# Gated linear attention and a max-out layer: a new opening, eight items transposed on PE, and matmuls on zeros in its gaps

## The chip, the cores and the metric

The kernel runs on one core of a Trainium2 chip. The metric is the device time of one execution in microseconds (us); the time before is the median of three runs, 171.43 us (169.94 to 171.87). The profile is of one execution of 170.57 us, whose span from first to last instruction is 168.3 us. PE is TensorE (matmuls), DVE VectorE, ACT ScalarE, POOL GpSimd, SP the engine whose queue issues all transfers.

## The reference

Inputs q, k, v and alpha have the shape (4, 8, 768, 48): 4 batches, 8 heads, 768 steps, head size 48, in float32. A gated linear attention runs over the steps, and its output of 3072 tokens x 384 goes through a max-out layer:

```python
for t in range(S):
    state = alpha[:, :, t, :, None] * state + np.einsum('bhd,bhe->bhde', k[:, :, t], v[:, :, t])
    y[:, :, t] = np.einsum('bhd,bhde->bhe', q[:, :, t], state)
x = np.ascontiguousarray(attn_out.transpose(0, 2, 1, 3)).reshape(B * S, H * D)
h1 = x @ w1      # w1, w2: 384 x 1024
h2 = x @ w2
g = np.maximum(h1, h2)
out = g @ w_out  # 1024 x 384
```

## The kernel before

**Items.** The attention works on 12 items, each 256 steps of one batch with all 8 heads; two steps lie side by side in a partition. An item loads alpha, q, k and v (384 KB each). ACT takes the logarithm of alpha (`ln`, L418), DVE adds the two steps (`su`, L425), PE forms running sums with triangular matrices (`cs`, L435 to L443), ACT takes exponentials (`en`, `ep`, `gg`), POOL multiplies k by en (`kt`, L474), DVE multiplies q (`qt`, L480), POOL casts v (`vc`, L489). Then q and k must be transposed. For the items in `TURN`, the first five, PE does that with 16 matmuls against the identity (L510) and ACT or DVE copies the result out of PSUM; for the other seven, two DMA transposes in the SP queue do it (L522). PE then forms the states (`kv`, L540), the scores (`sc`, L620); DVE masks them (`pt`, L628), PE forms y (L674) and ACT or DVE writes it to xT, transposed for the next layer (`xe`). DVE and POOL carry the states on from item to item (`w`, `T`, `t32`).

**Max-out.** max(h1, h2) is relu(x(w1 - w2)) + x w2, so the kernel keeps wd = w1 - w2 and m = w2 w_out, which PE computes once (L360, L392). Tokens come in chunks of 128; groups of 2 or 3 chunks go through `h` (L701, 24 matmuls with 256 or 384 columns), a relu each on ACT or DVE (L711, L709), and then for every chunk 3 matmuls with m (L726) and 8 with w_out (L728). An output chunk is evicted from PSUM (`ev`) and stored (`st`, L736).

**Order.** No loop fixes the order. All operations are handed to a planner (`Plan`, with `add` and `run`): each has a duration per engine it may run on, what it depends on, buffers it takes and releases, and a priority, where a smaller number goes first. `run` builds one fixed order per engine, which the chip then executes in order. Among the buffers are the 8 PSUM banks, in pairs ("A", for the attention) or singly ("M"). An operation of item n has a priority of about 100 n, a group g has 3000 + 100 g, so attention goes before groups. Loads have about -1000, stores -1500, DMA transposes -2000; all three share the SP queue. The planner limits how far ahead of the transfers SP issues (`LEAD`) and counts `xfer` us for each. Item 0 is loaded first, then the twelve loads of the weights (w2, w1, w_out in four pieces each), then items 1 to 11. There are 20 load buffers of 3 KB per partition and 6 output buffers.

Of the kernel before, what the change touches and what calls it, by code (L numbers as in the profile page):

```python
# [24 lines left out]
class Op:  # L25
    __slots__ = ("name", "engs", "emit", "deps", "takes", "uses", "prio", "mode", "xfer", "eng", "start", "end", "seen", "n")


class Plan:
# [4 lines left out]
    LEAD = 3.0  # L34

    def __init__(self, pools):
        self.free = dict(pools)
        self.banks = [True] * 8
        self.ops = []

    def room(self, takes):
        need = {}
        for b in takes:
            need[b.pool] = need.get(b.pool, 0) + 1
        for p, k in need.items():
            if p == "A":
                if self.pair() is None:
                    return False
            elif p == "M":
                if not any(self.banks):  # L50
                    return False
            elif self.free[p] < k:
                return False
        return True
# [7 lines left out]
    def take(self, b):  # L62
# [3 lines left out]
        elif b.pool == "M":  # L66
            free = [i for i in range(7, -1, -1) if self.banks[i]]
            half = [i for i in free if not self.banks[i ^ 1]]
            b.at = (half or free)[0]
            self.banks[b.at] = False  # L70
        else:
            self.free[b.pool] -= 1

    def give(self, b):
        if b.pool == "A":
            self.banks[b.at] = self.banks[b.at + 1] = True
        elif b.pool == "M":
            self.banks[b.at] = True
        else:
            self.free[b.pool] += 1  # L80

    def add(self, name, engs, emit, deps=(), takes=(), uses=(), prio=0.0, mode=None, xfer=0.0):
        o = Op()
        o.name, o.engs, o.emit, o.prio, o.mode, o.xfer = name, engs, emit, prio, mode, xfer
# [10 lines left out]
    def run(self):  # L95
        idle = {e: 0.0 for e in self.LAT}
        mode = None
        dma = 0.0
        order = []
# [3 lines left out]
        while waiting:  # L103
# [9 lines left out]
            for o in waiting:  # L113
# [6 lines left out]
                if ready is None:  # L120
# [6 lines left out]
                for e, dur in o.engs.items():  # L127
# [6 lines left out]
                    key = (o.prio, o.n)  # L134
                    if e not in best or key < best[e][0]:
                        best[e] = (key, o, dur)
            done = set()
            for e, (key, o, dur) in sorted(best.items(), key=lambda x: x[1][0]):
# [5 lines left out]
                if e == "PE" and o.mode != mode:  # L144
                    dur += self.SWITCH
                    mode = o.mode
# [3 lines left out]
                if e == "SP":  # L150
                    dma = max(dma, t + 1.3) + o.xfer
# [17 lines left out]
def kernel(  # L169
# [23 lines left out]
    WMAX = 384  # L193
    TURN = (0, 1, 2, 3, 4)
# [3 lines left out]
    NLD = 20  # L198
# [14 lines left out]
    plan = Plan({"ld": NLD, "en": 2, "loga": 2, "qk": 3, "pt": 4, "w": 4, "t32": 3, "gg": 3, "g": 2, "g16": 3, "outs": 6})  # L213
# [24 lines left out]
    def setup_pool1(eng):  # L238
        make_upper_triangular(nc, u16, val=1.0, diag=True)
        nc.gpsimd.memset(half1, 0.0)  # L240
# [7 lines left out]
        make_identity(nc, ident16)  # L248

    def setup_dve1(eng):  # L250
        nc.vector.memset(s16s[0][:, :, D:64], 0.0)
        nc.vector.memset(s16s[1][:, :, D:64], 0.0)
        nc.vector.tensor_sub(out=cmat, in0=u16, in1=half1)
        nc.vector.memset(cmat[0:64, 64:128], 0.0)
        nc.vector.tensor_sub(out=us16, in0=u16, in1=ident16)
        nc.vector.tensor_scalar_mul(out=nid16, in0=ident16, scalar1=-1.0)
        for i in range(2):
            nc.vector.memset(qkts[i].rearrange("p a j h d -> p (a j h) d")[:, :, D:64], 0.0)

    def setup_pool2(eng):  # L260
        for t in v16s:
            nc.gpsimd.memset(t.rearrange("p j h d -> p (j h) d")[:, :, D:96], 0.0)

    def setup_dve2(eng):
# [7 lines left out]
        nc.vector.memset(qkts[2].rearrange("p a j h d -> p (a j h) d")[:, :, D:64], 0.0)  # L272

    def setup_pool3(eng):
        for t in T16s:
            nc.gpsimd.memset(t, 0.0)

    s_p1 = plan.add("setp1", {"POOL": 2.6}, setup_pool1, prio=-100)
    s_d1 = plan.add("setd1", {"DVE": 2.6}, setup_dve1, deps=[s_p1], prio=-100)
    s_p2 = plan.add("setp2", {"POOL": 1.6}, setup_pool2, deps=[s_p1], prio=-90)  # L280
    s_d2 = plan.add("setd2", {"DVE": 1.3}, setup_dve2, deps=[s_d1], prio=-80)
    s_p3 = plan.add("setp3", {"POOL": 1.5}, setup_pool3, deps=[s_p2], prio=80)


    LX = 1024 * 20.5 / 16e3
    ld = {}

    def add_load(n, which, prio):
        src = {"a": alpha, "q": q, "k": k, "v": v}[which]
        b, c = divmod(n, NDB)  # L290
        buf = Buf("ld")

        def emit(eng):
            t = A["ld", n, which] = ldp.tile([128, H, 2 * D], FP32, tag="ld", name=which + "f")
            nc.sync.dma_start(  # L295
                out=t, in_=src[b, :, c * 256 : (c + 1) * 256, :].rearrange("h (p j) d -> p h (j d)", j=2)
            )

        ld[n, which] = (plan.add(f"ld{which}{n}", {"SP": 0.65}, emit, takes=[buf], prio=prio, xfer=LX), buf)

    WX = 384 * 1024 / 400e3
    wl = {}

    def add_wload(name, i, prio):
# [3 lines left out]
        def emit(eng):  # L308
            if name == "wo":
                t = ldp.tile([128, 2, DM], FP32, tag="ld", name="wof")  # L310
                nc.sync.dma_start(
                    out=t, in_=src[i * 256 : (i + 1) * 256, :].rearrange("(s p) d -> p s d", p=128)
                )
            else:
                t = ldp.tile([128, 3, 256], FP32, tag="ld", name=name + "f")
                nc.sync.dma_start(
                    out=t, in_=src.rearrange("(s p) f -> p s f", p=128)[:, :, i * 256 : (i + 1) * 256]
                )
            A["w", name, i] = t

        wl[name, i] = (plan.add(f"ld{name}{i}", {"SP": 0.5}, emit, takes=[buf], prio=prio, xfer=WX), buf)

    seq = [("d", 0)] + [("w2", i) for i in range(4)] + [("w1", i) for i in range(4)] + [("wo", i) for i in range(4)]
    seq += [("d", n) for n in range(1, ND)]
    pos = 0
    for name, i in seq:
        if name == "d":
            for w in "aqkv":
                add_load(i, w, -1000 + pos)
                pos += 1  # L330
        else:
            add_wload(name, i, -1000 + pos)
# [11 lines left out]
    w2c, wdc, woc, ptc = [], [], [], []  # L344
    for i in range(4):
        o, b = wl["w2", i]
        w2c.append(plan.add(
            f"w2c{i}", {"ACT": 0.83, "DVE": 0.55, "POOL": 1.25},
            lambda eng, i=i: cast(eng, w216[:, :, i * 256 : (i + 1) * 256], A["w", "w2", i]),
            deps=[o], uses=[b], prio=50 + i))  # L350

    for i in range(4):
        ps = Buf("M")

        def emit(eng, i=i, ps=ps):
            tp = A["wtp", i] = bank(ps, 384).bitcast(FP16).rearrange("p (u m) -> p u m", u=6)
            for u in range(2):
                for s in range(3):
                    f = 2 * i + u
                    nc.tensor.transpose(tp[:, 3 * u + s, :], w216[:, s, f * 128 : (f + 1) * 128], ident16)  # L360

        tr = plan.add(f"wtp{i}", {"PE": 0.34}, emit, deps=[w2c[i], s_p1], takes=[ps], prio=60 + i, mode=0)
        ptc.append(plan.add(
            f"wtc{i}", {"DVE": 0.6, "ACT": 0.8},
            lambda eng, i=i: cast(eng, w2T[:, 2 * i : 2 * i + 2, :].rearrange("p u m -> p (u m)"),
                                  A["wtp", i].rearrange("p u m -> p (u m)")),
            deps=[tr], uses=[ps], prio=61 + i))

    for i in range(4):
        o1, b1 = wl["w1", i]  # L370
        o2, b2 = wl["w2", i]

        def emit(eng, i=i):
            e = nc.vector if eng == "DVE" else nc.gpsimd
            e.tensor_sub(out=wd16[:, :, i * 256 : (i + 1) * 256], in0=A["w", "w1", i], in1=A["w", "w2", i])

        wdc.append(plan.add(f"wd{i}", {"DVE": 1.0, "POOL": 1.9}, emit, deps=[o1, o2], uses=[b1, b2], prio=70 + i))
    for i in range(4):
        o, b = wl["wo", i]
        woc.append(plan.add(  # L380
            f"woc{i}", {"ACT": 0.83, "DVE": 0.55, "POOL": 1.25},
            lambda eng, i=i: cast(eng, wo16[:, 2 * i : 2 * i + 2, :], A["w", "wo", i]),
            deps=[o], uses=[b], prio=74 + i))

    mc = []
    for s in range(3):
        ps = Buf("M")

        def emit(eng, s=s, ps=ps):
            mp = A["mp", s] = bank(ps, DM)  # L390
            for f in range(NF):
                nc.tensor.matmul(mp, lhsT=w2T[:, f, s * 128 : (s + 1) * 128], rhs=wo16[:, f, :],  # L392
                                 start=(f == 0), stop=(f == NF - 1))

        mm = plan.add(f"mp{s}", {"PE": 1.3}, emit, deps=ptc + woc, takes=[ps], prio=78 + s, mode=0)
        mc.append(plan.add(f"mc{s}", {"ACT": 0.48, "DVE": 0.5},
                           lambda eng, s=s: cast(eng, m16[:, s, :], A["mp", s]), deps=[mm], uses=[ps], prio=79 + s))
# [5 lines left out]
    def attention(n):  # L403
# [10 lines left out]
        loga_b = Buf("loga")  # L414

        def e_ln(eng):
            t = A["loga", n] = wk.tile([128, H, 2, D], FP16, tag="loga", name="loga")
# [367 lines left out]
```

## Time and profile before

| | busy us | share of span | instructions |
|---|---|---|---|
| PE | 134.8 | 80% | 2144 |
| DVE | 77.8 | 46% | 136 |
| ACT | 84.1 | 50% | 155 |
| POOL | 71.5 | 42% | 113 |

| view | what it says |
|---|---|
| chain that ended last | PE 49%, DMA 26%, DVE 7%, POOL 5% |
| SP queue | last input load issued at 103.4 us; 14 DMA transposes from 63.6 to 113.8 us |
| transfers | 23.59 MB read, 4.72 MB written |

The busy share of an engine is an average over the whole span. The rows with 40 digits cut the span into slices of 4.2 us, so that stages can be told apart. [...]matmuls overlap; what one costs in a stream is the distance from one start to the next.

### The profile page before, as it was taken

The page shows a single profiled execution, that of the slowest core. Times are in us where ns is not written, and L with a number is a line of the kernel's source. Part 1 is how long each engine was busy: PE and PEld are TensorE (multiplying, and loading weights), DVE is VectorE, ACT ScalarE, POOL GpSimd, SP SyncE. Part 2 cuts the span into 40 slices and gives each one's busy share as a digit, 9 for nine tenths or more (in the row PEclk, how much of TensorE's full clock was granted, in tenths as well). Part 3 has the DMA queues.
Part 4 walks back from the last instruction along what each step waited for, and adds up shares of the span by engine and source line. Part 5 has one row for each costly group of instructions (what it writes and reads, how often), then busy time and mean ns, then how long its engine had stood idle before and what let it go on. Part 6 is the DMA issues. An engine that isn't in the chain of part 4 may idle for free.

```text
span 168.3 us, 5032 instructions
## 1 busy us (share of the span) xinstructions
PE 134.8 (80%) x2144; PEld 89.6 (53%) x2144; DVE 77.8 (46%) x136; ACT 84.1 (50%) x155; POOL 71.5 (42%) x113
## 2 busy tenths in 40 slices
PE   0058599967884868969599894789989999999991
PEld 0047466745673645636256672545645666667660
DVE  3939922849678856618269564651930000001100
ACT  3255657453836549533563365262145482926342
POOL 7647900959794696781706467094100000000000
PEclk9999999999999699999879999699999999999999
DMA  5999999999999999999999999967210212103112
GB/s 142 265 346 348 370 280 238 274 247 266 310 241 277 251 257 247 197 268 246 200 237 208 235 254 219 263 78 156 90 51 0 93 47 76 68 25 117 47 47 93
DMA packets 72469, 32.29 MB, mean 192 GB/s; under 512 B 65280, under 2 KB 72448, under 8 KB 72448
## 3 DMA queue, kind: packets, MB, share of 16 engines
q1 hardware_dynamic: 72448, 31.99, 81.7%
q8 instruction: 16, 0.26, 0.7%
q14 instruction: 5, 0.04, 0.1%
HBM read 23.59 MB, written 4.72 MB: 168 GB/s over the span
## 4 chain that ended last, share of the span: by engine, by line
PE 49%; DMA 26%; DVE 7%; POOL 5%; SPq 4%; issue 4%; ACT 3%; DVEq 0%; ACTq 0%; POOLq 0%
PE PS L701 13%; PE PS L728 13%; DMA af<-in_alpha_dram 11%; DMA qk<-qkt 8%; PE PS L674 6%; PE PS L726 5%; DMA vf<-in_v_dram 4%; DMA w2f<-in_moe_w_dram 3%; PE PS L392 3%; SPq L295 3%; DVE pt L628 2%; PE PS L620 2%; POOL qkt L474 2%; PE PS L435 2%; PE PS L510 1%
## 5 line engine op out<-in xcount | busy, mean ns | idle before, releaser
L701 PE MATMUL PS<-xT,wd 128*128 128x384 f16 (+1 forms) x216 | 37.6, 319 | 3.9 <-ACT xT L338 2.6
L728 PE MATMUL PS<-wo,g 128*128 128x384 f16 x192 | 37.2, 326 | 0.0
L628 DVE TENSOR_TENSOR pt<-PS,mask 128x1024 f16<-128x1024 f32 x24 | 28.1, 1217 | 3.8 <-PE PS L620 3.5
L701 PEld LDWEIGHTS <-wd 128*128 128x128 f16 x216 | 20.3, 99 | 15.8 <-issue 4.7
L474 POOL TENSOR_TENSOR qkt<-kf,en 128x768 f16<-128x768 f32 x12 | 21.7, 1813 | 14.9 <-ACT gg L460 6.9
L711 ACT ACTIVATE g<-PS 128x384 f16<-128x384 f32 (+1 forms) x55 | 24.5, 458 | 6.3 <-PE PS L701 5.9
L709 DVE TENSOR_SCALAR g<-PS 128x384 f16<-128x384 f32 (+1 forms) x17 | 7.8, 493 | 37.8 <-PE PS L701 37.1
L338 ACT COPY outs<-PS 128x384 f32<-128x384 f32 x23 | 11.0, 478 | 28.2 <-PE PS L728 28.2
L728 PEld LDWEIGHTS <-g 128*128 128x128 f16 x192 | 18.1, 98 | 11.8 <-ACT g L711 0.2
L418 ACT ACTIVATE loga<-af 128x768 f16<-128x768 f32 x12 | 10.1, 843 | 18.8 <-DMA af<-in_alpha_dram 18.8
L620 PE MATMUL PS<-qk 48*64 48x128 f16 x384 | 9.5, 233 | 9.6 <-DMA qk<-qkt 5.1
L435 PE MATMUL PS<-s,cmat 128*128 128x384 f16 x24 | 8.4, 385 | 9.2 <-DVE s L425 8.5
L726 PE MATMUL PS<-m,xT 128*128 128x384 f16 x72 | 15.7, 326 | 0.0
L489 POOL CAST v<-vf 128x768 f16<-128x768 f32 x12 | 9.9, 823 | 13.0 <-DMA vf<-in_v_dram 12.8
L575 POOL TENSOR_TENSOR T<-w,gg 48x192 f16<-48x192 f32 x24 | 12.9, 539 | 4.3 <-DVE w L600 3.4
L620 PEld LDWEIGHTS <-qk 48*64 48x64 f16 x384 | 7.3, 115 | 13.1 <-issue 12.2
L480 DVE TENSOR_TENSOR qkt<-qf,PS 128x384 f16<-128x384 f32 x24 | 12.0, 546 | 4.0 <-DMA qk<-qkt 4.0
L452 ACT ACTIVATE en<-PS 128x768 f32<-128x768 f32 x12 | 9.7, 807 | 8.3 <-PE PS L443 8.1
L674 PE MATMUL PS<-pt,v 64*64 64x128 f16 x576 | 12.0, 233 | 0.1
L338 ACT CAST xT<-PS 128x384 f16<-128x384 f32 x13 | 7.6, 585 | 7.5 <-PE PS L701 4.5
L340 DVE CAST xT<-PS 128x384 f16<-128x384 f32 x11 | 6.5, 588 | 10.2 <-PE PS L701 5.4
L674 PEld LDWEIGHTS <-v 64*64 64x64 f16 x576 | 9.7, 116 | 1.6 <-issue 0.6
(66 smaller groups left out, 162.1 us busy)
## 6 DMA issues: line engine op xcount, KB each, us to landing
af<-in_alpha_dram SPq DMA_DIRECT2D x12, 384.0 KB, 6.1
qf<-in_q_dram SPq DMA_DIRECT2D x12, 384.0 KB, 5.8
kf<-in_k_dram SPq DMA_DIRECT2D x12, 384.0 KB, 5.7
vf<-in_v_dram SPq DMA_DIRECT2D x12, 384.0 KB, 6.0
out_dram<-outs SPq DMA_DIRECT2D x24, 192.0 KB, 1.9
w2f<-in_moe_w_dram SPq DMA_DIRECT2D x4, 384.0 KB, 5.9
w1f<-in_moe_w_dram SPq DMA_DIRECT2D x4, 384.0 KB, 7.8
wof<-in_moe_w_out_dram SPq DMA_DIRECT2D x4, 384.0 KB, 8.0
```

Of the source, the lines that this page charges most:

```text
L338: nc.scalar.copy(out=out, in_=in_)
L435: nc.tensor.matmul(t[:, g, 0:384], lhsT=cmat, rhs=s16[:, 4 * g : 4 * g + 4, 0:D].unsqueeze(2).to_broadcast([128, 4, 2, D]), start=True, st ...
L474: e.tensor_mul(out=hjd(qkts[i3], 1), in0=A["ld", n, "k"].rearrange("p h (j d) -> p h j d", j=2), in1=A["en", n].rearrange("p g (h j d) -> ...
L480: nc.vector.tensor_mul(out=hjd(qkts[i3], 0)[:, 4 * g : 4 * g + 4], in0=A["ld", n, "q"].rearrange("p h (j d) -> p h j d", j=2)[:, 4 * g : 4 ...
L575: e.tensor_mul(out=T16s[m % 4][o : o + 48, :, 48 * u : 48 * u + 48], in0=w_[o : o + 48], in1=g_[o : o + 48])
L620: nc.tensor.matmul(t[64 * x : 64 * x + 64, u, c0 : c0 + 128].rearrange("p (j m) -> p j m", j=2), lhsT=qk[o : o + D, 1, j, r, 64 * x : 64 * ...
L628: nc.vector.tensor_mul(out=t.rearrange("p u r c -> p (u r) c"), in0=A["sc", n, hf].rearrange("p u (r c) -> p (u r) c", r=2), in1=mask.rear ...
L674: nc.tensor.matmul(dst, lhsT=lhsT, rhs=rhs, start=(x, u) not in begun, stop=ends[x, u] == i, skip_group_check=True)
L701: nc.tensor.matmul(t[:, 0:W], lhsT=wd16[:, s, f * 128 : (f + 1) * 128], rhs=xT[:, s, a0 : a0 + W], start=(s == 0), stop=(s == 2))
L711: nc.scalar.activation(out=o, in_=i, func=ACTF.Relu)
L726: nc.tensor.matmul(A["op", t0], lhsT=xT[:, s, t0 : t0 + 128], rhs=m16[:, s, :], start=(s == 0), stop=False)
L728: nc.tensor.matmul(A["op", t0], lhsT=A["g16", g][:, f, i * 128 : (i + 1) * 128], rhs=wo16[:, f, :], start=False, stop=(f == NF - 1))
```

## The change

The change replaces the opening and retunes the planner:

- Items 0 to 7 are transposed on PE (`TURN`), items 8 to 11 by DMA.
- The weights come in six loads, w2, w_out and w1 by halves, between items 0, 1 and 2. Alpha and k share a load buffer, and so do q and v (10 buffers of 6 KB). m is built from two halves.
- Items 0 and 1 are worked in two halves of four heads (`SPLIT`), so that the first half can begin when half of alpha is there. Their k multiply is on DVE.
- Set-up work moves from POOL to DVE; the mask is built after the first sum.
- `FILL`: up to 60 matmuls on a tile of zeros, 128 x 512, with the lowest priority, which the planner may place where it foresees PE idle up to 24 us of its own count. Their result isn't used. They are there to keep PE's clock from falling to half. 55 of them are in the order of the built kernel.
- All groups have two chunks (`GROUPS`). Their priority is that of the item three later (`LAG`) instead of behind all attention. Stores go behind all loads (-100); there are 7 output buffers.
- In the planner, buffers are handed out in turn, PE is counted at half speed until it has been busy for 4 us (`WARM`), and several durations are set anew.

```diff
+TURN = (0, 1, 2, 3, 4, 5, 6, 7)
+SPLIT = (0, 1)
+LOADS = (0, ("w2", 0), ("wo", 0), ("w1", 0), 1, ("w2", 1), ("wo", 1), ("w1", 1), 2, 3, 4, 5, 6, 7, 8, 9, 10, 11)
+GROUPS = (2,) * 12
+LAG = 3.0
+FILL = (60, 24.0)
...
-    LEAD = 3.0
+    LEAD = 4.5
+    WARM = 4.0
...
-    TURN = (0, 1, 2, 3, 4)
...
-    NLD = 20
+    NLD = 10
...
-        for i in range(2):
-            nc.vector.memset(qkts[i].rearrange("p a j h d -> p (a j h) d")[:, :, D:64], 0.0)
-
-    def setup_pool2(eng):
-        for t in v16s:
-            nc.gpsimd.memset(t.rearrange("p j h d -> p (j h) d")[:, :, D:96], 0.0)
...
-    def setup_pool3(eng):
-        for t in T16s:
-            nc.gpsimd.memset(t, 0.0)
...
+    nfill, tfill = FILL
+    if nfill:
+        fz = constp.tile([128, 512], FP16)
+        fset = plan.add("fz", {"DVE": 0.2}, lambda eng: nc.vector.memset(fz, 0.0), prio=-120)
+        fb = Buf("M")
+        for i in range(nfill):
+            plan.add(f"fill{i}", {"PE": 0.21}, lambda eng: nc.tensor.matmul(bank(fb), lhsT=fz[:, 0:128], rhs=fz, start=True, stop=True,
+                                                                            skip_group_check=True),
+                     deps=[fset], takes=[] if i else [fb], uses=[fb] if i else [], prio=1e6 + i, mode=0, until=tfill)
...
-    LX = 1024 * 20.5 / 16e3
+    LX = 1024 * 25.5 / 16e3
...
+        split = n in SPLIT
+        parts = [(0, 4), (4, 8)] if split else [(0, 8)]
...
+            ke = {"DVE": 0.1 + 0.82 * F} if split else {"POOL": 0.1 + 1.72 * F}
...
-            ck = plan.add(f"dk{n}", {"SP": 1.2}, lambda eng: e_tr(eng, 1), deps=[kt], takes=[qkb], prio=-2000 + P, xfer=1.15)
...
+            cks.append(plan.add(f"dk{n}", {"SP": 1.2}, lambda eng: e_tr(eng, 1), deps=kts, takes=[qkb], prio=-2000 + P, xfer=1.6))
...
-        P = 3000 + 100 * g
+        P = 100.0 * ((c0 + nch - 1) // 2 + LAG)
...
-            plan.add(f"st{g}.{i}", {"SP": 0.65}, e_st, deps=[ev], uses=[ob], prio=-1500 + g, xfer=0.52)
+            plan.add(f"st{g}.{i}", {"SP": 0.65}, e_st, deps=[ev], uses=[ob], prio=-100 + g, xfer=0.52)
...
-    for g, nch in enumerate((2, 3, 3, 3, 3, 3, 3, 2, 2)):
+    for g, nch in enumerate(GROUPS):
```

## The prediction

> **What bounds the kernel now.** I read the slice rows of the page first, because a share over the whole span mixes stages here.
>
> ```profile
> PE   0058599967884868969599894789989999999991
> PEclk9999999999999699999879999699999999999999
> GB/s 142 265 346 348 370 280 238 274 247 266 310 241 277 251 257 247 197 268 246 200 237 208 235 254 219 263 78 156 90 51 0 93 47 76 68 25 117 47 47 93
> ```
>
> A slice is 4.2 us. Up to slice 26 (109 us) the DMA engines move 200 to 370 GB/s without a pause and PE has gaps; after that hardly anything is moved and PE is full. So there are two stages: until about 118 us PE is fed by transfers, then it works off a backlog. The stretches and waits (name, total us, times, longest) say the same:
>
> ```profile
> 8.50:30.00 21.50, 17.31 (x216) 12.71 (x216) 11.85 (x19) 13.58 (x20) 9.79 (x8) 1.00 1.10 315
> ...
> 118.00:165.00 47.00, 45.80 (x443) 28.93 (x431) 6.60 (x8) 23.41 (x54) 0.32 (x1) 1.00 0.16 58
> ```
>
> ```profile
> ACT loga L418 <- DMA af<-in_alpha_dram: 18.8, 12, 3.4
> ...
> PE PS L435 <- DVE s L425: 8.5, 1, 8.5
> ...
> PE PS L620 <- DMA qk<-qkt: 5.1, 3, 3.1
> ```
>
> ACT waits 18.8 us for alpha; PE waits 8.5 us once at the start and 5.1 us for the DMA transposes. The chain that ended last has these in the middle of the run:
>
> ```profile
> 62.00 6.75 DMA af<-in_alpha_dram
> ...
> 87.96 7.05 DMA qk<-qkt
> ...
> 100.26 5.76 DMA qk<-qkt
> ...
> 134.29 3.41 PE PS L701 x21
> ```
>
> Alpha and the transposed q and k take turns as the last releaser: both go through the one SP queue. The last line gives a price: 21 matmuls of 384 columns in 3.41 us, 0.163 us each.
>
> **How much PE work there is.** I priced PE's matmuls by their start-to-start times in undisturbed places of the timeline: 384 columns 0.163 us, 256 columns 0.109 (21 in 2.29), a score set of 32 0.57, a y of 16+48 matmuls 1.37, a state set of 32 0.37, a transpose 0.062 (16 in 1.0), a decay block (L435, L438, L443) 0.66. Summed over the kernel before this is 118.6 us, of a span of 168.3. By that scale PE does 45.5 us of work from 117.6 to 164.9 (rate 0.96), but from 61.6 to 102.9 only 32.4 (0.785), and from 27.6 to 117.6 only 64.0 of 90 (0.71). About 26 us of the span are lost in that 90 us stretch; that is what a change of staging can win.
>
> [...] L435 starts 0.32 us apart from its follower at 8.5, 55.5, 83.6 and 107.4 us, and 0.16 where PE was busy before. [...] The inputs' rows are 384 B, and the trace has 346 to 370 GB/s while weights move and about 263 (mean of slices 7 to 14) while inputs do. [...]
>
> **The change part by part.**
>
> *Transposes.* Items 5, 6 and 7 move from DMA to PE. Removed: 6 of 14 DMA transposes (1.4 us each in the SP queue, 4.3 us to landing), and with the new order the other 8 all come after the last load. Added: 48 PE transposes x 0.062 = 3.0 us of PE, and 6 copies of 0.68 (DVE) or 1.01 us (ACT), about 5 us on engines that are 46% and 50% busy. PE's sum becomes 121.7 us.
>
> *Loads.* The bytes are the same (23.6 MB). In before 8.25 MB stand ahead of and with item 2's alpha, which landed at 30.5; the new order has the same bytes there, so 30.5 again. It needs ln 0.84, sum 0.40 and some 0.5 of hand-overs: item 2's decay matmuls can start at 32.3. After that nothing but loads is on the queue: 1.573 MB an item at 263 GB/s is 6.0 us, item 3 at 38.3, item 11 at 86, where before still issued loads at 103.
>
> *Stores.* The instruction order has the first store behind all 54 input issues, and 7 output buffers. Chunk 7 (the eighth) has 55.4 us of PE work ahead of it: 32.3 + 39.7 = 72 at full rate; item 11's alpha lands near 84.5, its v 4.5 us later, and a load is issued some 6 us before it lands (the median of before): the last near 83, the first store behind it. So from 72 to about 85 finished chunks wait in PSUM: 7, then 8 (62.2 of work, 79), 9 and perhaps 10, up to four banks of eight: a new wait, longer by what the loads are late. Behind the waiting evictions stand the relus on ACT and DVE, and PE waits for those. I cost it at 0 to 6 us.
>
> *Groups of two items' chunks.* 288 matmuls of 256 columns (31.4 us) replace 144 of 384 and 72 of 256 (31.3): nothing. 96 relus of 0.38 to 0.42 for 72 of 0.38 to 0.56: 38 for 34 us on ACT and DVE, beside PE.
>
> *Priority.* A group's work now stands by the item three later, not behind all attention: in PE's order 15.7 us of work are ahead of item 2, then 22.7, 31.3, 37.1, 46.5, 56.0 ahead of items 3 to 7. An item is about 9.7 us of PE work ((121.7 - 5.4 for the weights)/12) against 6.0 of loading. So after item 2 the loads run ahead: item 3 is allowed at 38.3 and is reached at 39.3 at the earliest; by item 6 the slack is 63.1 against 56.3.
>
> *Opening.* Splitting items 0 and 1, the multiplies by en on DVE (two 1.81 us POOL operations become four of about 0.55 us on DVE), weights in six transfers, set-up moved from POOL to DVE (before's took until 8.05, with one DVE operation on 128x128 lasting 3.78 us): all of it ends ahead of item 2 at 32.3, which waits for its bytes, so on the path it is worth nothing by itself, but it must fit: 15.7 of work and 55 matmuls on zeros[...]. They are in PE's fixed order, so data that come earlier than the order foresees wait behind some of them[...]. Their use is a warm clock; cold stretches of before in the opening cost PE 2 to 3 us that were hidden.
>
> *Sum.* End = 32.3 + (108.0 - 15.7)/r + 13.7 + 3.4 + 2.3. 108.0 is the work up to item 11's y, 13.7 what follows and runs at full rate as in before, 3.4 the tail from the last matmul to the span's end (164.9 to 168.3), 2.3 the difference of time and span. r is PE's rate while attention and groups mix: the one unknown. Undisturbed stretches of before give 0.83 (61.6 to 73.7), 0.97 (95.1 to 102.9), 0.96 (from 117.6). With a backlog three items deep I take 0.93: 51.7 + 99.2 = 150.9, said as 151.
>
> **The rivals.** *A. Hand-overs or held PSUM banks (r 0.80 to 0.87).* For it: PE waits for xT, pt and qk copies in before, 0.3 to 2.1 us each, and the queue of stores. Against: an item costs DVE 4.6 us (sum 0.40, q 1.1, masks 2.4, states 0.7), ACT 2.6 (ln, two exps, gg) and either of them 7.1 (copies of q and k 1.7, xT 1.2, relus 3.2, outputs 1.0): 7.2 each, against PE's 9.7. Time 158 to 167. *B. Slower.* If before's mixed stage is slow because of the hand-overs between engines and not because of DMA, r stays at 0.71: 51.7 + 130 = 182; even 0.76 gives 173. Against: the chain has DMA where PE waits longest. *C. Better than thought.* r 0.98 or more and item 2's bytes 2 us earlier[...]: 142 to 145. *D. The gain is hidden anyway*, because PE works off a backlog at the end in both: but the sum of PE work is 118.6 against 168.3, so idle time is on the path.
>
> **Numbers.** The main case (146 to 157) 0.62, A 0.22, C 0.07, B 0.09 (a sliver of A and B falls within 1%). Range 144 to 165: it leaves out B, the far end of A and half of C. Faster 0.88, same 0.03, slower 0.09.
>
> **What would show it.** PE's digits at 9 from slice 8 on; no alpha or qk landing among PE's or the chain's long pieces after 33 us; last load issued by 88; no cold L521 after 35 us; item 2's decay matmuls at 31 to 34. Wrong if PE idles over 15 us after 33, if ACT or DVE stands waiting for stores around 75 to 92 with PE behind it, or if item 2 starts after 36.

## The result, and the profile after

The changed kernel takes 152.6 us, the median of four runs (152.01 to 153.17), against 171.35 us for the kernel before on the same chip: a ratio of 0.892, 95% interval 0.885 to 0.899. The ratios of this document leave out runs over 1.5% above the fastest of the same kernel; the medians include them. The profiled run's span is 151.3 us. The slices are now 3.78 us wide:

```profile
PE   6999989699999999999998988999989699999991
PEclk9999999999999999999999999999999999999999
GB/s 117 272 333 375 258 245 366 304 246 269 268 252 247 267 244 261 210 262 236 234 252 217 276 263 145 311 254 153 176 61 98 88 74 123 56 0 108 101 3 104
```

PE is at 90% or more in all but nine of the 40 slices, in the opening partly with the matmuls on zeros, and the clock row shows no slice in which the clock is lowered: its mean is 1.000 (the trace records it from 5.3 us on only; before that a matmul on zeros takes 0.42 us, right after it 0.22, as shown below). The transfers move 210 to 276 GB/s in most slices up to 90 us, as before: the same bytes at the same pace, but PE has far fewer gaps while they come. The three stretches that the prediction's sum speaks of (length, PE, PEld, DVE, ACT, POOL with instructions, clock, DMA share, GB/s):

```profile
8.50:34.10 25.60, 23.09 (x392) 15.38 (x392) 20.46 (x38) 15.14 (x31) 11.10 (x16) 1.00 1.04 306
34.10:134.20 100.10, 95.85 (x1800) 69.32 (x1798) 64.00 (x114) 55.94 (x113) 51.41 (x74) 1.00 0.84 200
134.20:148.10 13.90, 13.84 (x103) 9.58 (x99) 3.99 (x9) 5.67 (x13) 0.00 (x0) 1.00 0.16 58
```

The waits of PE from 33 us on (us in total, times, longest) are all that is left of before's:

```profile
PE PS L787 <- DVE xT L400: 1.7, 3, 0.6
PE PS L787 <- ACT xT L398: 1.2, 2, 0.7
PE PS L787 <- ACT g L797: 0.5, 1, 0.5
PE PS L787 <- DVE pt L714: 0.3, 1, 0.3
PE PS L760 <- issue: 0.2, 1, 0.2
```

That is 3.9 us, none of it on a transfer. In the kernel before, PE waited 5.1 us for the transposes alone. Of ACT's twelve waits for a load of alpha, 18.8 us before, one is left, for the first load of all. The chain that ended last has no DMA in its shares of the span (second fence):

```profile
ACT loga L502 <- DMA ldf<-in_alpha_dram: 1.5, 1, 1.5
```

```profile
PE 87%; DVE 6%; ACT 2%; issue 1%; POOL 1%; ACTq 0%; POOLq 0%
```

### The profile page after: what moved, and what is told of

The parts are those of the page before. It is cut to its first block, busy times and chain, and to the rows that moved or that the text cites. A ratio compares the mean times of both kernels' runs of the same rounds, so it can differ in the third digit from the quotient of the medians.

```text
span 151.3 us, 5429 instructions
## 1 busy us (share of the span) xinstructions
PE 140.1 (93%) x2319; PEld 97.4 (64%) x2319; DVE 94.4 (62%) x187; ACT 82.0 (54%) x167; POOL 64.6 (43%) x106
## 4 chain that ended last, share of the span: by engine, by line
PE 87%; DVE 6%; ACT 2%; issue 1%; POOL 1%; ACTq 0%; POOLq 0%
PE PS L787 22%; PE PS L814 21%; PE PS L760 10%; PE PS L812 8%; PE PS L328 7%; PE PS L585 5%; PE PS L706 4%; PE PS L521 3%; PE PS L626 2%; DVE wd L436 2%; DVE pt L714 1%; PE PS L446 1%; PE PS L524 1%; DVE xT L400 1%; POOL T L661 1%
## 5 line engine op out<-in xcount | busy, mean ns | idle before, releaser
L787 PE MATMUL PS<-xT,wd 128*128 128x256 f16 x288 | 38.4, 273 | 4.1 <-DVE xT L400 1.7
L787 PEld LDWEIGHTS <-wd 128*128 128x128 f16 x288 | 26.4, 97 | 10.5 <-issue 4.9
L797 ACT ACTIVATE g<-PS 128x256 f16<-128x256 f32 x57 | 20.9, 384 | 18.0 <-PE PS L787 17.8
L559 POOL TENSOR_TENSOR qkt<-ldf,en 128x768 f16<-128x768 f32 x10 | 18.1, 1814 | 23.4 <-issue 11.6
L795 DVE TENSOR_SCALAR g<-PS 128x256 f16<-128x256 f32 x39 | 16.2, 421 | 13.3 <-PE PS L787 13.0
L328 PE MATMUL PS<-fz 128*128 128x512 f16 x55 | 16.8, 421 | 1.2 <-DVE fz L325 1.2
L565 DVE TENSOR_TENSOR qkt<-ldf,PS 128x384 f16<-128x384 f32 x24 | 12.1, 547 | 3.9 <-ACT PS L543 3.3
L398 ACT CAST xT<-PS 128x384 f16<-128x384 f32 x12 | 7.0, 591 | 12.2 <-PE PS L760 9.9
L575 POOL CAST v<-ldf 128x768 f16<-128x768 f32 (+1 forms) x14 | 10.4, 753 | 7.1 <-DMA ldf<-in_v_dram 6.8
L539 ACT ACTIVATE en<-PS 128x768 f32<-128x768 f32 (+1 forms) x14 | 10.1, 720 | 5.5 <-PE PS L529 4.5
L502 ACT ACTIVATE loga<-ldf 128x768 f16<-128x768 f32 (+1 forms) x14 | 10.5, 751 | 1.6 <-DMA ldf<-in_alpha_dram 1.5
L585 PE MATMUL PS<-ident,qkt 128*128 128x128 f16 x128 | 10.4, 219 | 0.2 <-ACT qk L398 0.2
```

Of the source, the lines that this page charges most:

```text
L328: plan.add(f"fill{i}", {"PE": 0.21}, lambda eng: nc.tensor.matmul(bank(fb), lhsT=fz[:, 0:128], rhs=fz, start=True, stop=True, skip_group_c ...
L398: nc.scalar.copy(out=out, in_=in_)
L559: e.tensor_mul(out=hjd(qkts[i3], 1)[:, hd], in0=A["ld", n, "k"][:, hd].rearrange("p h (j d) -> p h j d", j=2), in1=A["en", n][:, g0:g1].re ...
L585: nc.tensor.transpose(A["tp", n][:, a, r, j, :], src[:, j, r, :], ident16)
L787: nc.tensor.matmul(t[:, 0:W], lhsT=wd16[:, s, f * 128 : (f + 1) * 128], rhs=xT[:, s, a0 : a0 + W], start=(s == 0), stop=(s == 2))
L795: nc.vector.tensor_relu(o, i)
```

## The experiments

Ratios are to the kernel before, timed beside it on the same chip, with 95% intervals. The experiments ran on three chips, on which the median of before was 171.8, 171.2 and 173.4 us, so kernels of different chips are compared by ratio. All the kernels compute the full output.

**Four parts taken out of the changed kernel.** First, no matmuls on zeros:

```diff
-FILL = (60, 24.0)
+FILL = (0, 24.0)
```

> The changed kernel with no matmuls on zeros; all else the same. My step: they lie in gaps and are worth nothing on the path beyond a warm clock in the opening; item 2's decay matmuls (L521) stay at 33.5 to 35.5 us and the time at 152 to 155. Rival 'clock': without them the opening runs at half clock, item 2 starts at 37 or later, and the time is 156 or more. Rival 'in the way': they are 7.3% of the chain that ended last, real work queues behind them, and without them the time falls to 150 or less.

Measured 152.1 us, ratio 0.888 (0.880 to 0.895). What the zeros do can be read from PE's first instructions in the changed kernel (start, us, instruction, count, idle before):

```profile
1.20 4.02 PE L328 MATMUL PS<-fz 128*128 128x512 f16 x9 [1.20 <-DVE fz L325]
5.01 0.45 PE L521 MATMUL PS<-s,cmat 128*128 128x384 f16 x1
...
5.44 1.24 PE L328 MATMUL PS<-fz 128*128 128x512 f16 x5
```

and without them:

```profile
4.46 0.48 PE L521 MATMUL PS<-s,cmat 128*128 128x384 f16 x1 [4.46 <-DVE s L510]
```

Without zeros the first real matmul starts 0.55 us earlier. It is cold in both kernels (0.28 and 0.29 us to its follower, against 0.16 warm); the second L521 is warm with zeros, at 6.52 us (0.16 to its follower), and cold without, at 5.40 (0.28). Item 2 starts at 35.60 us without zeros, 34.06 with them, but also at 35.45 in the run with stores ahead of loads (below), which has the zeros and the same order in the opening. The time is the same (0.888 without zeros, 0.892 with them): they bring the warm pace earlier and are worth nothing that can be measured.

Second, the transposes of items 5 to 7 back in the SP queue:

```diff
-TURN = (0, 1, 2, 3, 4, 5, 6, 7)
+TURN = (0, 1, 2, 3, 4)
```

> The changed kernel with items 5, 6 and 7 transposed by DMA again (PE work 118.7 instead of 121.7 us). My theory: the transposes stand in the one queue with the loads and hold them up, waits of PE for q and k come back, and the time is 155 to 162 although PE has 3.0 us less to do. Rival: with loads three items ahead nothing waits for them, and the time falls by the 3.0 us, to 149 to 150.

Measured 159.24 us, 0.926 (0.917 to 0.935). SP's queue shows what transposes do to the loads behind them (start, time in the queue, instruction, count):

```profile
60.12 2.67 SPq L606 DMA_TRANSPOSE qk<-qkt  x1
...
68.12 4.19 SPq L606 DMA_TRANSPOSE qk<-qkt  x2
...
82.17 5.33 SPq L606 DMA_TRANSPOSE qk<-qkt  x2
87.56 0.57 SPq L358 DMA_DIRECT2D ldf<-in_v_dram  x1
```

The five transposes of these lines hold the queue for 12.2 us, 2.4 each on average. The load right behind one takes 0.57, but that is no fair price of a load: the median of this run's loads is 1.3 us, and its 14 transposes take 2.1 on average (29.6 in all). What counts is that eight transposes, 18.4 us in the queue together, now stand ahead of the last load. It is issued at 99.2 us instead of 86.7, and PE has gaps at 80 to 110 us. In this kernel the transposes on PE are worth about 4%.

Third, the groups' priority behind all attention:

```diff
-        P = 100.0 * ((c0 + nch - 1) // 2 + LAG)
+        P = 3000 + 100 * g
```

> The changed kernel with the groups' old priority, behind all attention. PE's order is the same up to item 5; after it items 6 to 11 have 45.3, 52.5, 59.8, 60.8, 68.0 and 69.8 us of PE work ahead of them instead of 46.5, 56.0, 66.6, 77.6, 83.1 and 91.3. Theory 'backlog': loads still arrive ahead of PE (item 11's at about 88 us against 88), so the time is 152 to 157. Rival 'priority is the change': attention comes to its limit of loads again as in before, PE idles, and the time is 160 or more.

Measured 155.92 us, 0.910 (0.903 to 0.916): in this kernel the priority is worth about 2%.

Fourth, stores ahead of the loads again:

```diff
-            plan.add(f"st{g}.{i}", {"SP": 0.65}, e_st, deps=[ev], uses=[ob], prio=-100 + g, xfer=0.52)
+            plan.add(f"st{g}.{i}", {"SP": 0.65}, e_st, deps=[ev], uses=[ob], prio=-1500 + g, xfer=0.52)
```

> The changed kernel with the stores' old priority, ahead of the loads. I costed the held output chunks at 0 to 6 us. If they hold PE up, the time falls to 147 to 151. If the banks were never short, it stays within 1 us of 152.6. Rival: a store in the queue that waits for its eviction holds up the loads behind it, and the time is 155 or more.

Measured 152.66 us, 0.890 (0.884 to 0.897): nothing. Held PSUM banks cost the changed kernel no time that can be measured, and its trace has no wait for them.

**Parts put into the kernel before.** If transposes and priority are the cause, the kernel before with them must come near the new one. Transposes alone (`TURN` of items 0 to 7), priority alone, and both:

```diff
-    TURN = (0, 1, 2, 3, 4)
+    TURN = (0, 1, 2, 3, 4, 5, 6, 7)
...
-        P = 3000 + 100 * g
+        P = 100.0 * ((c0 + nch - 1) // 2 + 3.0)
```

> The kernel before with items 5, 6 and 7 transposed on PE, nothing else. If the transposes in the load queue are what held it (the second run says 6.6 us of the changed kernel), the loads come through earlier and the time falls to 161 to 166, but all attention still goes first, so PE has only 52 us of work ahead of item 11 and keeps idling until its alpha comes. Rival 'PE price': the 3.0 us added to PE come out on the path, and the time is 171 to 175. Rival 'transposes are all of it': 156 or less.

Measured 169.93 us, 0.992 (0.988 to 0.995).

> The kernel before with the groups' new priority (by the item three later), nothing else; transposes stay on DMA. In PE's order items 6, 9 and 11 now have 42, 71 and 83 us of work ahead of them instead of 32, 48 and 65. Theory: the queue still holds loads and transposes, so PE catches up with the loads and waits: 163 to 170. Rival 'priority is the change': 158 or less.

Measured 168.85 us, 0.985 (0.978 to 0.993).

> The kernel before with both: eight items on PE and the new priority; the old opening, the old groups, the old durations in the planner, no matmuls on zeros. My sum has nothing for the opening: in before item 2's decay matmuls start at 32.8 us with 14.2 us of work done (18.6 apart), in the changed kernel at 34.1 with 15.7 (18.4). So this should come to 152 to 156. Rival 'opening': without the new opening the time stays at 160 or more.

Measured 165.59 us, 0.965 (0.959 to 0.971): a third of the gain. The two parts on which the prediction put the gain do not make it. A further kernel has both, and also the durations that the new planner counts with: a load lasts 1.63 us instead of 1.31, a DMA transpose 1.6 instead of 1.15, and SP may run 4.5 us ahead instead of 3.0.

```diff
-    LEAD = 3.0
+    LEAD = 4.5
...
-    LX = 1024 * 20.5 / 16e3
+    LX = 1024 * 25.5 / 16e3
...
-            ck = plan.add(f"dk{n}", {"SP": 1.2}, lambda eng: e_tr(eng, 1), deps=[kt], takes=[qkb], prio=-2000 + P, xfer=1.15)
+            ck = plan.add(f"dk{n}", {"SP": 1.2}, lambda eng: e_tr(eng, 1), deps=[kt], takes=[qkb], prio=-2000 + P, xfer=1.6)
```

> As the run before it (eight items on PE, new priority, old opening), and with the planner's durations for transfers as in the change: 1.63 us a load, 1.6 us a DMA transpose, SP 4.5 us ahead. If the old durations make PE's order wait for loads that the planner thinks are there, this is 2 us or more faster than the run with both alone, at 151 to 154. If not, within 1 us of it.

Measured 156.34 us, 0.911 (0.904 to 0.917). These are numbers in the planner alone. They add no work; what they change is the fixed order on each engine and, for some copies and relus, which of ACT and DVE runs them (ACT 151 and DVE 146 instructions here, 148 and 149 in the kernel with both parts alone). So the next two kernels change `LX` and `LEAD` alone, in both directions. The kernel before with the new ones:

```diff
-    LEAD = 3.0
+    LEAD = 4.5
...
-    LX = 1024 * 20.5 / 16e3
+    LX = 1024 * 25.5 / 16e3
```

> The kernel before with only the new durations for input loads (1.63 us, SP 4.5 us ahead); items 5 to 11 on DMA and the old priority stay. If late data in the order was half of the loss by itself, the time falls by about 9 us, to 160 to 164. If it pays only once the transposes are out of the queue and groups lie between the items, it stays at 167 to 171.

Measured 156.82 us, 0.904 (0.897 to 0.911), far more than either theory gave it. PE's and POOL's instructions are as many as before (2144 and 113); on balance six copies and relus have moved from ACT to DVE. With 14 DMA transposes in the load queue and groups behind all attention, this kernel has nine tenths of the gain. PE still waits for the transposes as long as before (5.1 us then):

```profile
PE PS L620 <- DMA qk<-qkt: 4.8, 4, 2.3
```

ACT's wait for alpha, though, is 7.4 us instead of 18.8. Nor do the loads come sooner: the last is issued at 111.7 us, 103.4 before. From 30 to 60 and from 60 to 90 us the kernel before did

```profile
30.00:60.00 30.00, 23.10 (x563) 17.25 (x561) 22.76 (x41) 15.68 (x27) 22.62 (x33) 0.94 1.11 265
...
60.00:90.00 30.00, 24.67 (x426) 15.39 (x424) 16.11 (x29) 16.73 (x32) 16.14 (x26) 0.94 1.17 239
```

and with the two constants

```profile
30.00:60.00 30.00, 27.64 (x605) 19.94 (x603) 25.47 (x46) 21.04 (x34) 23.39 (x35) 1.00 1.07 257
...
60.00:90.00 30.00, 26.05 (x497) 16.41 (x497) 17.14 (x30) 15.47 (x29) 16.42 (x25) 1.00 1.20 236
```

The transfers bring no more bytes (257 and 236 GB/s against 265 and 239), yet PE is busy for 5.9 us longer in these 60 us (4.54 + 1.38) and runs 113 matmuls more. PE's clock is a small part of that at most: over the whole span it is 0.978 of full speed on average, 0.969 before. In the first of the two stretches the additional matmuls are those of the groups. Of L701 and L728 PE ran from 30 to 60 us, before,

```profile
30.00:60.00 30.00, 2.04 (x13) 0.94 1.11 265
...
30.00:60.00 30.00, 3.26 (x16) 0.94 1.11 265
```

and with the two constants

```profile
30.00:60.00 30.00, 6.51 (x41) 1.00 1.07 257
...
30.00:60.00 30.00, 6.04 (x32) 1.00 1.07 257
```

With L726 (6 and 12) the groups' matmuls go from 35 to 85, at a time when both kernels still put all attention first: a planner that expects alpha later sees a gap on PE and fills it with group work, where the old order let PE stand. From 60 to 90 us the groups have 84 and 97, and most of the rest is attention that is further on.

POOL shows one more place. Before:

```profile
35.56 0.82 POOL L489 CAST v<-vf 128x768 f16<-128x768 f32 x1 [1.84 <-DMA vf<-in_v_dram]
36.35 0.51 POOL L587 TENSOR_TENSOR t<-w,gg 112x192 f32<-112x192 f32 x1
36.82 1.09 POOL L575 TENSOR_TENSOR T<-w,gg 48x192 f16<-48x192 f32 x2
37.99 1.81 POOL L474 TENSOR_TENSOR qkt<-kf,en 128x768 f16<-128x768 f32 x1
```

With the two constants:

```profile
34.90 0.52 POOL L587 TENSOR_TENSOR t<-w,gg 112x192 f32<-112x192 f32 x1 [0.33 <-DVE w L600]
35.37 1.09 POOL L575 TENSOR_TENSOR T<-w,gg 48x192 f16<-48x192 f32 x2
36.54 1.81 POOL L474 TENSOR_TENSOR qkt<-kf,en 128x768 f16<-128x768 f32 x1
38.32 0.20 POOL L553 TENSOR_TENSOR g<-gg 112x4 f32<-112x4 f32 x1
38.46 0.82 POOL L489 CAST v<-vf 128x768 f16<-128x768 f32 x1
```

Both casts are of item 2's v. With the short duration the planner counts on v at 29.4 us and puts its cast ahead of the state updates and the multiply by en. On the chip v lands at 35.4, POOL stands, and what is behind the cast stands too. With the longer one the cast is behind them and waits for nothing. This is one place in some 90 us. POOL's total wait for v is no shorter (12.8 us before, 13.4 with the two constants); what got shorter is ACT's wait for alpha. Two things were not tried: `LX` and `LEAD` apart from each other, and other values of them.

The reverse, the changed kernel with the old constants (`LX` of 20.5, `LEAD` of 3.0):

> The changed kernel with the planner's old durations for input loads (1.31 us for 1.63, SP 3.0 us ahead for 4.5), all else new. Theory 'order built on late data': an engine's fixed order puts an instruction that still waits for its load ahead of work that is ready, as POOL's cast of v in the old kernel; the time rises by 3 to 9 us, to 156 to 162. Rival 'backlog absorbs it': with transposes and stores out of the queue and PE three items behind the loads, nothing on the path waits for a load, and the time stays within 1 us of 152.6.

Measured 161.83 us, 0.928 (0.919 to 0.937). The waits for loads come back, 1.5 us for alpha and 6.8 for v in the changed kernel:

```profile
POOL v L575 <- DMA ldf<-in_v_dram: 19.1, 7, 6.9
...
ACT loga L502 <- DMA ldf<-in_alpha_dram: 9.1, 7, 2.5
```

But the largest loss is of another kind. PE and ACT have a wait that the changed kernel lacks:

```profile
PE PS L812 <- ACT outs L398: 5.6, 1, 5.6
...
ACT outs L398 <- DMA out_dram<-outs: 7.1, 1, 7.1
```

It is one event. In the timeline of all engines:

```profile
89.09 6.50 SPq L822 DMA_DIRECT2D out_dram<-outs  x9
94.18 1.05 ACT L398 COPY outs<-PS 128x384 f32<-128x384 f32 x2 [7.08 <-DMA out_dram<-outs]
94.71 1.12 PE L812 MATMUL PS<-m,xT 128*128 128x384 f16 x3 [5.60 <-ACT outs L398]
```

No output is stored before all loads are issued (89.09 us). All output buffers are full, ACT can't evict the next chunk, and PE waits for the bank. This is the wait that the prediction bounded at 0 to 6 us; it appears at 5.6 when the planner counts on earlier loads. A second loss lies in the opening: item 2's first L521 is at 37.45 us, not at 34.1. Its alpha landed at 32.26 and its logarithm ran at once; then DVE's sum stands behind a copy to xT that waits for PE, and PE behind matmuls that wait for wd, whose weights landed at 31.0 us and take POOL 2.5 us more.

How far the planner is from the chip can be read for every kernel, because `run` gives each operation a time at which its result is there (`seen`). For the landing of item 11's alpha, in us:

| kernel | planner | chip | late by | ratio |
|---|---|---|---|---|
| before | 86.2 | 103.0 | 16.8 | 1 |
| before, transposes and priority | 75.3 | 88.5 | 13.1 | 0.965 |
| before, two constants | 103.2 | 108.5 | 5.3 | 0.904 |
| before, both parts and new durations | 91.3 | 93.4 | 2.1 | 0.911 |
| changed, old constants | 73.8 | 89.3 | 15.5 | 0.928 |
| changed | 88.2 | 88.5 | 0.3 | 0.892 |

In each of the three pairs the kernel whose planner is nearer to the chip is faster, though its alpha lands 5 us later in the first two and 0.8 us sooner in the third.

**Groups and split.** On the same chip as the last two, the changed kernel with the old nine groups, and with no split of items 0 and 1:

```diff
-GROUPS = (2,) * 12
+GROUPS = (2, 3, 3, 3, 3, 3, 3, 2, 2)
```

> The changed kernel with the nine groups of before (2, 3, 3, 3, 3, 3, 3, 2, 2 chunks). I costed the groups of two at nothing: 152 to 153.5. Rival: groups of three wait for two items, PE's backlog comes later and in larger pieces, and 2 to 4 us of the 3.7 that lie between the old opening with both changes and durations (156.3) and the changed kernel (152.6) are theirs: 154.5 to 157.

Measured 155.02 us with before at 173.4, 0.894 (0.888 to 0.901): the same as the changed kernel. The microseconds fall where the rival put them, but on this chip the kernel before is slower too.

```diff
-SPLIT = (0, 1)
+SPLIT = ()
```

> The changed kernel with items 0 and 1 worked whole. I costed the split at nothing on the path, since item 2 waits for its bytes in any case: 152 to 153.5. Rival: the split is what lets PE finish item 0 and 1 ahead of the weights, and without it the time is 154.5 or more.

Measured 150.77 us with before at 173.4, 0.871 (0.865 to 0.877): the fastest of all, and on one chip 4.3 us under the kernel with nine groups, which times like the changed one. The gain is not in the opening, where item 2 starts at 35.9 us after 17.6 us of the work that the prediction priced: 18.3 us of it are lost, as with the split (34.1 us less 15.7, 18.4). It is in the stage after it:

```profile
35.90:132.00 96.10, 94.25 (x1788) 68.19 (x1787) 62.23 (x112) 57.93 (x115) 50.45 (x73) 1.00 0.90 202
```

From item 2 to item 11 PE did 73.4 us of work in 77.5 us, a rate of 0.947, against 75.6 in 81.3 (0.930) in the changed kernel. No wait of the changed kernel in that stage belongs to the split. Without the split the k multiply of items 0 and 1 is also back on POOL. That the planner's order merely came out better, by more than groups, stores or zeros are worth, is our reading and not shown.

## Why the prediction was right in its time and wrong in its cause

**The sum.** It said 32.3 + 92.3/0.93 + 13.7 + 3.4 + 2.3. Measured: 34.1 to item 2's decay matmuls, 100.1 for the same 92.3 of work (r = 0.922), 13.9 after item 11's y, 3.2 from the last matmul to the end, and 1.3 between the profiled span and the median. The largest miss of a term is 1.8 us, at item 2. But r was called the one unknown, and 0.93 was taken for the backlog that transposes and priority would build. Counted with the prediction's prices from item 2's start to item 11's y, r is 0.71 in before and 0.83 with these two parts; with 0.83 the same sum gives 163 us. It is 0.87 with the two constants alone, and 0.92 with parts and durations together. That 0.93 came out is therefore in part luck: it needed durations of which the prediction didn't speak.

**Item 2's start.** "The same bytes, so 30.5 again" was short by 0.6: its alpha, issued at 20.60 us, landed at 31.10. ACT's logarithm of it ran at 31.80 without waiting for DMA, right behind copies of item 1 to xT:

```profile
30.91 1.05 ACT L398 CAST xT<-PS 128x384 f16<-128x384 f32 x2 [0.94 <-PE PS L760]
31.80 0.85 ACT L502 ACTIVATE loga<-ldf 128x768 f16<-128x768 f32 x1
```

After it DVE's sum came at 33.43, behind a copy of m. So in this execution 1.2 of the 1.8 us are hand-overs, and "all of it ends ahead of item 2 at 32.3" was wrong by that much. It isn't so in every execution: in the run with stores ahead of loads, with the same order up to there, alpha landed at 33.38, its logarithm followed at once, and item 2 started at 35.45. Bytes and hand-overs end close together, and the start moves by 1.4 us with the transfers.

**The rest of the change.** From the kernel before with both parts and new durations to the changed kernel the ratio goes from 0.911 to 0.892, intervals apart, so what is left (opening, groups, stores, other durations) brings some 2%. Of the 3.6 us between the two profiled spans (154.9 and 151.3) 2.3 lie ahead of item 2: 20.6 us of PE's time are lost there against 18.3, at the prediction's prices. As that start moves by 1.4 us by itself, this is a hint that the opening has a worth, no more; which part brings the 2% is open.

**Pace of the loads.** "6.0 us an item" was short. Alphas are issued at 43.52 to 82.25 us for six items, 6.46 each, or 1.6 us a load; the last load was issued at 86.67 (predicted 83). The backlog took it up: no alpha, v or transpose is waited for by PE.

**Rate 0.93 and rival B.** B (r stays at 0.71) is out. A is out too: r is above its 0.80 to 0.87, and the waits of PE for xT, g and pt sum to 3.7 us. C needed r of 0.98; even the best kernel had 0.947. The price list, with matmuls by their start-to-start distance, holds: in the changed kernel twelve of 384 columns (L446, from 30.79 us) take 1.96 us from the first start to the start of what follows, 0.163 each, and twelve of 256 (L787, from 39.92) 1.31, 0.109 each. Their durations in the profile overlap and are longer, 0.33 and 0.27 us on average.

**The step that failed: which part brings it.** The prediction gave the gain to the transposes that leave the load queue and to the priority, and priced groups and opening at nothing on the path. It put the planner's new durations at nothing by not naming them. In the kernel before, transposes and priority together are worth 3.5%, the duration of a load and the lead alone 9.6%, and with these in place adding both (and the new duration of a transpose) changed nothing measurable (0.911 with them, 0.904 without, intervals overlapping). The chain of before, read as "both go through the one SP queue", was also the picture of engines that had been ordered to wait. These pieces were in it (start, us, what), and were passed over:

```profile
29.06 6.39 DMA vf<-in_v_dram
...
35.56 0.82 POOL v L489
36.39 0.47 POOL t L587
36.86 0.47 POOL T L575
...
37.99 1.82 POOL qkt L474
```

The load is followed by the cast, and the cast by work that doesn't need this v. What runs next is what the planner thinks is ready: with 1.31 us for a load against 1.6 measured, its count runs ahead of the chip by about 4 x 0.3 = 1.2 us with each item, an estimate. In before the landing of alpha is 5.0 us late against the planner at item 2 (30.5 for 25.5), 10.7 at item 8 and 16.8 at item 11.

**Parts are not additive.** In the changed kernel, undoing transposes costs 3.8%, the durations 4.1%, the priority 2.0% (ratios of the ratios above), though in the kernel before transposes brought 0.8% and priority 1.5%. That the transposes matter in the changed kernel, where the stores come after all loads and so a late load delays them, is argued, not shown. The intervals of the kernel before with the two constants (0.904) and of the changed one (0.892) just overlap.

**Zeros.** A matmul on zeros takes 0.216 us warm (five from 5.44 to 6.52 us) and 0.42 cold (nine from 1.20 to 5.01). A clock at half speed is in the trace of before: the granted clock is 0.50 from 83.4 to 84.4 us, where L435 starts 0.32 us ahead of its follower, and 1.00 from 61.5 to 62.6, where it starts 0.16 to 0.17 ahead. The "warm clock" that the prediction gave as their use is there (mean 1.000 in the changed kernel, 0.977 without zeros), and is worth nothing that can be measured. That they fit ahead of item 2 was the author's estimate; item 2 starts at 34.06 us with them and at 35.60 without.

**Stores.** "0 to 6 us" held at both ends: 0 in the changed kernel, 5.6 in the same kernel with the old durations. The stores stood behind all loads in both, so their place alone doesn't decide which.

## What to carry to other kernels

When a planner fixes the order of in-order engines, look at the durations it counts with before its parts: measure the pace of transfers in a trace, put that number in, and compare the planner's landing times with the chip's. A wait for a transfer in the chain may mean that the transfer is late, or that the order put its consumer ahead of work that was ready; look at what stands behind the waiting instruction. And test a cause by adding it to the old kernel as well as by taking it out of the new one: here the transposes on PE were worth 4% in one and 1% in the other.

## What the runs showed that was not expected

Two constants of a planner, with no work added and with loads that land later, brought 9.6%. Leaving out the split, a part that was meant to help the opening, brought 2.3% more in a stage long after it. So orders of this kernel that differ by little in the planner differ by some per cent on the chip, and an effect of 2% of one part is not safely that part's own. The three pairs in the table differ by 4.1 to 9.6%, all the same way.
